# Strided values on shifted partitions, loaded in two pieces, and token rows stored tile by tile: a kernel of strided and local attention with a mixture of experts

## The chip, the cores and the metric

One core of a Trainium2 chip runs the whole program. The metric is the device time of one execution in microseconds. Of the kernel before, three runs gave 592.94, 595.64 and 595.68 us: the median is 595.64 us.

## The reference

Eight batches with eight heads of 576 tokens, 64 elements a head. The first four heads attend to the 32 latest tokens; the last four to earlier tokens of the same residue modulo 32 (18 of them). The 4608 token rows of 512 elements then go through a mixture of eight experts; each row goes to the one expert with the largest gate.

```python
scores = scale * np.matmul(q, k.transpose(0, 1, 3, 2))
rel = pos[:, None] - pos[None, :]
mask_local = (rel >= 0) & (rel < stride)
mask_strided = (rel >= 0) & (pos[None, :] % stride == pos[:, None] % stride)
...
attn = attn / (np.sum(attn, axis=-1, keepdims=True) + 1e-09)
return np.matmul(attn, v).astype(np.float32)
...
x = np.ascontiguousarray(attn_out.transpose(0, 2, 1, 3)).reshape(B * S, H * D)
logits = x @ w_gate + modality_bias[modality_id]
e_idx = np.argmax(logits, axis=1)
...
    h = np.maximum(x[mask] @ w1[e], 0.0)
    out[mask] = gate_w[mask, None] * (h @ w2[e])
```

## The kernel before

The work is cut into 32 units, eight for each of four pairs of batches, in turn a `Local` one (one local head of two batches) and a `Strided` one (two strided heads of one batch). A step n of the main loop (L1105) works on several units at once: the scores of unit n, the transposes (`turn`) of unit n - 2, the matmuls with the values (`values`) of unit n - 3, and in the middle of these the loads for later units. So each step has one unit of one kind in `scores`, and two steps make a pair with all loads of both kinds.

All loads of attention are issued by SP, in the order of the loop: for a local unit two pieces of `qk` (queries and keys) and two of `vv` (values), for a strided unit two pieces of `qks` and one load of `vs`. Each load of 128 partitions has 288 to 304 KB, and `vs` has 72 partitions with 4 KB each, 288 KB. `after_landing` (L777) makes a load wait until a matmul of the running step is done, so that not all loads are on their way at once: the second piece of `qk` or `qks` waits for the scores of the step, the first piece of the values for its transposes, the second piece for its value matmuls. `load_values(1)` of a strided unit loads nothing before the change.

In a strided unit a row of the values' matrix is a token of a residue: the matmul (L470) multiplies 72 rows, 18 tokens of each of four residues, of `vs` with `eb`. `eb` holds the transposed probabilities `en`, once for each residue and each time multiplied by a column of 0 and 1 from the constants `cf` (columns `C_T`), so that a residue meets its own 18 rows only (L453 to L460).

When the eight units of a pair are through, `finish_pair` (L480) transposes the results into token rows `xt` (nine tiles of 128 tokens), routes them, and stores them into `xd` in DRAM, from where the experts gather their tokens. For the first two pairs (`EARLY`) the stores go to the list `stores` and are issued by POOL (`store_rows`, L518), one per step of the main loop; for the other two pairs ACT issues them at once. `in_turn` (L780) keeps POOL's transfers in one order and makes each wait for a recent result of the units.

TensorE's order is written out by hand (`manual_schedule`, L1102); a scheduler orders the other engines by due times. The main loop ends near 165 us of the span. Behind it, and interleaved with the last units, the experts' feed-forward runs over slots of 384 tokens (`ffn`, L959), with split matmuls (`wh`, `wl`).

The loop's lines around the change are:

```python
        if 1 <= n <= nu:
            ins = units[n - 1].load_values(0)
            if n >= 2:
                after_landing(ins, units[n - 2].point)
...
        if n >= 3:
            units[n - 3].values()
        if 1 <= n <= nu:
            ins = units[n - 1].load_values(1)
            if ins and n >= 3:
                after_landing(ins, units[n - 3].valued)
```

Of the kernel before, what the change touches and what calls it, by code (L numbers as in the profile page):

```python
# [11 lines left out]
F32 = mybir.dt.float32  # L12
# [8 lines left out]
P = 128  # L21
# [24 lines left out]
TURNED = 4  # L46
EARLY, BEGIN = 2, 28
BIG = -float(2 ** 30)
SKIP = 2 ** 16
# [6 lines left out]
C_T = C_P + 1  # L56
C_F = C_T + 4
C_H = C_F + 4
# [26 lines left out]
def _constants():  # L85
# [6 lines left out]
    cf[:, C_F:C_F + 4] = P * np.arange(4)  # L92
    for t in range(4):
        cf[18 * t:18 * t + 18, C_T + t] = 1
    cb = np.zeros((P, M_N), np.float32)
# [88 lines left out]
def attention_moe(ctx: ExitStack, tc: tile.TileContext, a, out):  # L184
# [105 lines left out]
    for t in qzs:  # L290
        nc.gpsimd.memset(t[:], 0.0)


# [97 lines left out]
    class Strided:  # L391
# [11 lines left out]
        def load_values(self, part):  # L403
            if part == 0:
                self.vs = lp.tile([72, 8, 2, D], F32, tag="vs", name=f"vs{self.n}")
                return pin(nc.sync.dma_start(
                    self.vs.rearrange("p g h d -> p (g h d)"), a["vs"][self.b, self.pr]))

# [11 lines left out]
        def scores(self):  # L420
# [23 lines left out]
            nc.vector.reciprocal(sm[:], sm[:])  # L444
            self.en = lp.tile([P, 16, 18], F32, tag="ens", name=f"ens{n}")
            spots.append(nc.vector.tensor_tensor(self.en[:], ex[:], bc(sm), ALU.mult))

        def turn(self):
            n = self.n
            tp = pa(f"ts{n}").rearrange("p (g q) -> p g q", g=4)  # L450
            for g in range(4):
                self.point = turned_to(tp[0:72, g, :], self.en[:, 4 * g:4 * g + 4, :])
            self.eb = eb = lp.tile([72, 8, 4, 36], F32, tag="eb", name=f"eb{n}")  # L453
            src = tp[0:72].rearrange("p g (j x) -> p (g j) x", j=2)[:, :, 0:36]
            sh = [72, 8, 2, 36]
            nc.vector.tensor_tensor(
                eb[:, :, 0:2, :], src.unsqueeze(2).to_broadcast(sh),
                cf[0:72, C_T:C_T + 2].unsqueeze(1).unsqueeze(3).to_broadcast(sh), ALU.mult)
            for t in (2, 3):
                nc.scalar.activation(eb[:, :, t, :], src, AF.Copy, scale=cf[0:72, C_T + t:C_T + t + 1])  # L460

        def values(self):
            n, eb, vs, b = self.n, self.eb, self.vs, self.b
            for g2 in range(2):
                ot = pa(f"ot{n}{g2}")[:, :288]
                for g in (2 * g2, 2 * g2 + 1):
                    for j in range(2):
                        c = (g % 2) * 144 + 72 * j
                        for h in range(2):
                            self.valued = nc.tensor.matmul(  # L470
                                ot[64 * h:64 * h + 64, c:c + 72],
                                vs[:, 2 * g + j, h, :],
                                eb[:, 2 * g + j, :, 18 * h:18 * h + 18],
                                start=True, stop=True, skip_group_check=True,
                            )
                base = (b % 2) * S
                dst = self.xc[:, base:base + S].rearrange("p (q r) -> p r q", r=32)[:, 16 * g2:16 * g2 + 16, :]
                mark(nc.scalar.copy(dst, ot.rearrange("p (r q) -> p r q", r=16)))

    def finish_pair(bp, xt, xcs):  # L480
# [22 lines left out]
        for k0 in (0, 4, 8):  # L503
# [5 lines left out]
            if bp < EARLY:  # L509
                for k1 in range(k0, k0 + kn, 2):  # L510
                    stores.append(partial(store_rows, bp, xt, k1, min(2, 9 - k1)))
            else:
# [592 lines left out]
    for n in range(nu + 3):  # L1105
# [29 lines left out]
        pop(POPS)  # L1135
        if stores:
            stores.pop(0)()
        if n >= BEGIN:
# [75 lines left out]
```

## Time and profile before

| | |
|---|---|
| runs | 592.94, 595.64, 595.68 us |
| profiled execution | 598.07 us, span 596.3 us |
| TensorE busy | 570.7 us, 96% |
| VectorE (DVE), ScalarE (ACT), GpSimd (POOL) busy | 383.9, 328.8, 203.5 us |
| mean granted TensorE clock | 0.992 |
| moved by DMA | 103.50 MB, mean 174 GB/s |

Busy time counts neither the issue of DMAs nor waits. The time of the profiled execution includes 1.77 us around the span. In a timeline a row stands for several like instructions, and what is in brackets is the time in which the engine did nothing before the row, and what ended it. "issue" there means that the profile shows nothing for which the engine waited. SPq, ACTq and POOLq stand for instructions that issue DMAs.

### The profile page before, as it was taken

The numbers are of one execution on the slowest core, as the hardware profiler recorded it, in microseconds if no ns is written. First come the engines' busy times: TensorE is split into PE (matmuls) and PEld (weight loads), VectorE is DVE, ScalarE is ACT, GpSimd is POOL, SyncE is SP. The second block draws the span as 40 slices with busy tenths as digits, with TensorE's granted clock in tenths as the row PEclk, the third lists the DMA queues.
The fourth block names the chain that finished last, engine by engine and source line by source line (L and its number), as shares of the span: only waits on it lengthen the run. The fifth ranks groups of instructions, "written<-read, shape, count | busy, mean of one in ns | idle before, by whom it ended". The sixth has DMA issues, their size and how long they took to land.

```text
span 596.3 us, 13716 instructions
## 1 busy us (share of the span) xinstructions
PE 570.7 (96%) x5461; PEld 504.6 (85%) x5461; DVE 383.9 (64%) x925; ACT 328.8 (55%) x656; POOL 203.5 (34%) x194
## 2 busy tenths in 40 slices
PE   9889789889899999999999999999999999999995
PEld 5778777777789889899999898999989998998984
DVE  6885967966776795456476666657476666655432
ACT  5698878867574353445454454545454454545442
POOL 3010201102654326532264545544433444423121
PEclk9999999989899999999999999999999999999999
DMA  8997987968868515645555155432414256423421
GB/s 278 304 269 229 340 261 237 341 209 276 274 238 314 169 62 178 221 171 190 142 195 107 53 195 141 146 72 70 90 35 107 53 195 162 154 54 107 158 89 56
DMA packets 59547, 103.50 MB, mean 174 GB/s; under 512 B 33427, under 2 KB 33683, under 8 KB 55380
## 3 DMA queue, kind: packets, MB, share of 16 engines
q0 software_dynamic: 15904, 57.47, 28.2%
q1 hardware_dynamic: 40692, 39.85, 23.6%
q10 hardware_dynamic: 2880, 5.23, 2.5%
q8 instruction: 45, 0.74, 0.5%
q14 instruction: 26, 0.21, 0.1%
HBM read 98.28 MB, written 19.18 MB: 197 GB/s over the span
## 4 chain that ended last, share of the span: by engine, by line
PE 88%; issue 4%; DMA 4%; ACT 2%; POOL 1%; DVE 1%; POOLq 0%; ACTq 0%
PE h L968 34%; PE o L982 33%; DMA vs<-in_vs 3%; PE s L338 2%; PE ot L470 2%; PE ss L425 2%; PE o L373 2%; PE xs L217 2%; PE lg L532 1%; PE warm L204 1%; PE t L217 1%; PE xl L217 1%; PE xt L217 1%; DMA le<-ld,li 1%; PE ts L217 1%
## 5 line engine op out<-in xcount | busy, mean ns | idle before, releaser
L1004 DVE TENSOR_TENSOR wl<-raw,wh 128x512 fp32r<-128x512 f32 x192 | 126.3, 696 | 84.9 <-ACT wh L1003 78.1
L1003 ACT CAST wh<-raw 128x512 fp32r<-128x512 f32 x192 | 109.7, 622 | 115.2 <-PE o L982 101.2
L968 PE MATMUL h<-xh,wl 128*128 128x384 f32 x384 | 129.5, 337 | 0.0
L968 PE MATMUL h<-xl,wh 128*128 128x384 f32 x384 | 129.0, 336 | 0.0
L968 PE MATMUL h<-xh,wh 128*128 128x384 f32 x384 | 128.1, 337 | 0.3 <-ACT wh L1003 0.3
L982 PE MATMUL o<-wh,hl 128*128 128x512 f32 x288 | 113.7, 395 | 0.0
L982 PE MATMUL o<-wl,hh 128*128 128x512 f32 x288 | 113.5, 394 | 0.0
L982 PE MATMUL o<-wh,hh 128*128 128x512 f32 x288 | 112.8, 392 | 0.0
L971 ACT ACTIVATE hh<-h 128x384 fp32r<-128x384 f32 x96 | 47.2, 492 | 87.0 <-PE h L968 73.2
L973 DVE SCALAR_TENSOR_TENSOR hl<-h,hh 128x384 fp32r<-128x384 f32 x96 | 53.4, 556 | 57.5 <-ACT hh L971 57.1
L836 POOL DMA_INDIRECT raw<-in_w,wi x48 | 55.7, 1160 | 75.7 <-ACT hh L971 65.6
L968 PEld LDWEIGHTS h<-xh,wh 128*128 128x128 f32 x384 | 72.1, 188 | 4.4 <-ACT wh L1003 0.5
L968 PEld LDWEIGHTS h<-xl,wh 128*128 128x128 f32 x384 | 72.1, 188 | 3.7 <-issue 0.4
L804 POOL DMA_INDIRECT fx<-xd,le x36 | 44.3, 1231 | 82.0 <-DMA work<-work 21.4
L968 PEld LDWEIGHTS h<-xh,wl 128*128 128x128 f32 x384 | 72.0, 188 | 0.0
L982 PEld LDWEIGHTS o<-wh,hl 128*128 128x128 f32 x288 | 54.0, 188 | 11.5
L982 PEld LDWEIGHTS o<-wl,hh 128*128 128x128 f32 x288 | 54.1, 188 | 9.3
L982 PEld LDWEIGHTS o<-wh,hh 128*128 128x128 f32 x288 | 54.1, 188 | 8.9
L821 POOL DMA_INDIRECT le<-ld,li x36 | 39.0, 1082 | 58.1 <-DVE lo L565 26.0
L990 POOL DMA_INDIRECT out<-y,le x36 | 37.3, 1037 | 43.9 <-ACT y L989 37.6
L931 DVE COPY work<-fx 128x1536 uint16<-128x1536 uint16 x16 | 27.2, 1745 | 2.1 <-DMA fx<-xd,le 2.1
L524 POOL DMA_DIRECT2D xd<-xt x10 | 7.2, 725 | 62.1 <-ACT xt L487 39.9
(192 smaller groups left out, 771.2 us busy)
## 6 DMA issues: line engine op xcount, KB each, us to landing
vv<-in_vl SPq DMA_DIRECT2D x32, 292.5 KB
qks<-in_qks SPq DMA_DIRECT2D x32, 288.0 KB
qk<-in_qkl SPq DMA_DIRECT2D x16, 304.0 KB
qk<-in_qkl SPq DMA_DIRECT2D x16, 288.0 KB
vs<-in_vs SPq DMA_DIRECT2D x16, 288.0 KB
xd<-xt POOLq DMA_DIRECT2D x8, 512.0 KB
xd<-xt ACTq DMA_DIRECT2D x4, 1024.0 KB
raw<-in_w,wi POOLq DMA_INDIRECT x48
```

Of the source, the lines that this page charges most:

```text
L217: return nc.tensor.transpose(dst, src, ident)
L804: ins = in_turn(nc.gpsimd.indirect_dma_start(xt[:, h, :], None, xd[0:xrows, :], IOA(ap=le[:, h, 0:1], axis=0), **bounds))
L821: in_turn(nc.gpsimd.indirect_dma_start(le[:, h, :], None, ld[0:1 + last, :], IOA(ap=li[:, s, h:h + 1], axis=0)))
L836: ins = nc.gpsimd.indirect_dma_start(raws[j].rearrange("p f c -> p (f c)"), None, a["w"], IOA(ap=wi[:, s, j:j + 1], axis=0), bounds_check= ...
L931: pin(nc.vector.tensor_copy(rows[:, :, w, :], halves(xt)[:, :, :, w]))
L968: nc.tensor.matmul(hp, w[:, a1], x[:, c, :], start=(k == 0), stop=(k == 11))
L971: steps.append(nc.scalar.activation(hh[:], hp, AF.Relu))
L973: nc.vector.scalar_tensor_tensor(hl[:], hp, 0.0, hh.bitcast(F32), ALU.max, ALU.subtract)
L982: nc.tensor.matmul(os[h], hx[:, m], w[:, 512:1024], start=(f == 0 and i == 0), stop=(f == 7 and i == 2))
L990: outs.add(in_turn(nc.gpsimd.indirect_dma_start(out, IOA(ap=le[:, h, 0:1], axis=0), y[:], None, bounds_check=NT - 1, oob_is_err=False), True))
L1003: nc.scalar.copy(wh[:, c], raw[:, c])
L1004: nc.vector.tensor_tensor(wl[:, c], raw[:, c], wh[:, c].bitcast(F32), ALU.subtract)
```

## The change

Three things change. The values `vs` of a strided unit no longer lie on partitions 0 to 71 but on 32 to 103 in even strided units and on 24 to 95 in odd ones (`ROWS`), in two fixed buffers `vsp`. They are loaded by two DMAs: 64 rows on partitions 32 to 95, issued where the one load stood, and the other 8 rows on 96 to 103 or 24 to 31, issued behind the value matmuls of the step.

So that the probabilities lie on the same partitions, `en` is written into a buffer `enp` with 32 columns of zeros ahead of it, and the transpose takes 104 or 96 columns from there. `eb` and the matmul go over 104 or 96 partitions; the masks in `cf` are 0 in the rows ahead, and the buffers are set to zero by POOL at the start.

The token rows of the first two pairs are stored tile by tile, nine stores of 256 KB instead of four of 512 KB and one of 256 KB, one per step and two in each fourth step.

```diff
@@ -45,6 +45,7 @@
 WHEN = {1: 0, 3: 1, 5: 2, 7: 3}
 TURNED = 4
 EARLY, BEGIN = 2, 28
+ROWS = 32, 24
 BIG = -float(2 ** 30)
 SKIP = 2 ** 16
 
@@ -54,7 +55,7 @@
 C_SIO = C_RE8 + E
 C_P = C_SIO + NBP * LA
 C_T = C_P + 1
-C_F = C_T + 4
+C_F = C_T + 8
 C_H = C_F + 4
 C_N = C_H + TH
 
@@ -90,8 +91,9 @@
     cf[:, C_SIO:C_SIO + NBP * LA] = np.arange(NBP * LA)
     cf[:, C_P] = np.arange(P)
     cf[:, C_F:C_F + 4] = P * np.arange(4)
-    for t in range(4):
-        cf[18 * t:18 * t + 18, C_T + t] = 1
+    for i, r0 in enumerate(ROWS):
+        for t in range(4):
+            cf[r0 + 18 * t:r0 + 18 * t + 18, C_T + 4 * i + t] = 1
     cb = np.zeros((P, M_N), np.float32)
     cb[:, M_ID:M_ID + P] = np.eye(P)
     qi = np.arange(32)[:, None]
@@ -288,6 +290,10 @@
     for t in qds + ets:
         nc.vector.memset(t[:], 0.0)
     for t in qzs:
+        nc.gpsimd.memset(t[:], 0.0)
+    enp = zeros(2, [P, 32 + 288], "enp")
+    vsp = zeros(2, [104, 8, 2, D], "vsp")
+    for t in vsp + enp:
         nc.gpsimd.memset(t[:], 0.0)
 
 
@@ -401,10 +407,11 @@
             return pin(nc.sync.dma_start(self.qk[:, part, :], a["qks"][self.b, self.pr, :, S * part:S * part + S]))
 
         def load_values(self, part):
-            if part == 0:
-                self.vs = lp.tile([72, 8, 2, D], F32, tag="vs", name=f"vs{self.n}")
-                return pin(nc.sync.dma_start(
-                    self.vs.rearrange("p g h d -> p (g h d)"), a["vs"][self.b, self.pr]))
+            r0 = ROWS[self.n % 2]
+            r = (32, 96) if part == 0 else (96, 104) if r0 == 32 else (24, 32)
+            return pin(nc.sync.dma_start(
+                vsp[self.n % 2].rearrange("p g h d -> p (g h d)")[r[0]:r[1]],
+                a["vs"][self.b, self.pr, r[0] - r0:r[1] - r0]))
 
         def prep(self):
             self.qz = qz = qzs[self.n % 2]
@@ -442,25 +449,30 @@
             nc.vector.tensor_reduce(sm[:], ex[:], AX.X, ALU.add)
             nc.vector.tensor_scalar(sm[:], sm[:], 1e-9, None, ALU.add)
             nc.vector.reciprocal(sm[:], sm[:])
-            self.en = lp.tile([P, 16, 18], F32, tag="ens", name=f"ens{n}")
-            spots.append(nc.vector.tensor_tensor(self.en[:], ex[:], bc(sm), ALU.mult))
+            self.en = enp[n % 2]
+            spots.append(nc.vector.tensor_tensor(
+                self.en[:, 32:320].rearrange("p (i k) -> p i k", i=16), ex[:], bc(sm), ALU.mult))
 
         def turn(self):
-            n = self.n
+            n, r0 = self.n, ROWS[self.n % 2]
+            kn = r0 + 72
             tp = pa(f"ts{n}").rearrange("p (g q) -> p g q", g=4)
             for g in range(4):
-                self.point = turned_to(tp[0:72, g, :], self.en[:, 4 * g:4 * g + 4, :])
-            self.eb = eb = lp.tile([72, 8, 4, 36], F32, tag="eb", name=f"eb{n}")
-            src = tp[0:72].rearrange("p g (j x) -> p (g j) x", j=2)[:, :, 0:36]
-            sh = [72, 8, 2, 36]
+                c0 = 32 + 72 * g
+                self.point = turned_to(tp[0:kn, g, :], self.en[:, c0 - r0:c0 + 72])
+            self.eb = eb = lp.tile([104, 8, 4, 36], F32, tag="eb", name=f"eb{n}")
+            src = tp[0:kn].rearrange("p g (j x) -> p (g j) x", j=2)[:, :, 0:36]
+            sh = [kn, 8, 2, 36]
+            c0 = C_T + 4 * (n % 2)
             nc.vector.tensor_tensor(
-                eb[:, :, 0:2, :], src.unsqueeze(2).to_broadcast(sh),
-                cf[0:72, C_T:C_T + 2].unsqueeze(1).unsqueeze(3).to_broadcast(sh), ALU.mult)
+                eb[0:kn, :, 0:2, :], src.unsqueeze(2).to_broadcast(sh),
+                cf[0:kn, c0:c0 + 2].unsqueeze(1).unsqueeze(3).to_broadcast(sh), ALU.mult)
             for t in (2, 3):
-                nc.scalar.activation(eb[:, :, t, :], src, AF.Copy, scale=cf[0:72, C_T + t:C_T + t + 1])
+                nc.scalar.activation(eb[0:kn, :, t, :], src, AF.Copy, scale=cf[0:kn, c0 + t:c0 + t + 1])
 
         def values(self):
-            n, eb, vs, b = self.n, self.eb, self.vs, self.b
+            n, eb, vs, b = self.n, self.eb, vsp[self.n % 2], self.b
+            kn = ROWS[n % 2] + 72
             for g2 in range(2):
                 ot = pa(f"ot{n}{g2}")[:, :288]
                 for g in (2 * g2, 2 * g2 + 1):
@@ -469,8 +481,8 @@
                         for h in range(2):
                             self.valued = nc.tensor.matmul(
                                 ot[64 * h:64 * h + 64, c:c + 72],
-                                vs[:, 2 * g + j, h, :],
-                                eb[:, 2 * g + j, :, 18 * h:18 * h + 18],
+                                vs[0:kn, 2 * g + j, h, :],
+                                eb[0:kn, 2 * g + j, :, 18 * h:18 * h + 18],
                                 start=True, stop=True, skip_group_check=True,
                             )
                 base = (b % 2) * S
@@ -507,8 +519,8 @@
                 rows_of(c, k0)
             kn = min(4, 9 - k0)
             if bp < EARLY:
-                for k1 in range(k0, k0 + kn, 2):
-                    stores.append(partial(store_rows, bp, xt, k1, min(2, 9 - k1)))
+                for k1 in range(k0, k0 + kn):
+                    stores.append(partial(store_rows, bp, xt, k1, 1))
             else:
                 store_rows(bp, xt, k0, kn, nc.scalar)
         yield from routing
@@ -1133,8 +1145,9 @@
         if n + 2 < nu:
             units[n + 2].prep()
         pop(POPS)
-        if stores:
-            stores.pop(0)()
+        for _ in range(1 if n % 4 else 2):
+            if stores:
+                stores.pop(0)()
         if n >= BEGIN:
             issue(2)
         if n == nu + 1:
```

On SP, after the start-up the order of one pair of steps is this (`qk`, `vv`: the local unit's, `qks`, `vs`: the strided unit's; the DMAHW names are the eight counters of landed transfers, used in turn). Before:

```order
L406 DMA vs_765<-in_vs 72x1024 [waits DMAHW0_49,PE_49]
L305 DMA qk_791<-in_qkl 128x576 [waits DMAHW1_49,DVE_49,Activation_49]
L305 DMA qk_791<-in_qkl 128x608 [waits DMAHW2_49,PE_49]
L313 DMA vv_846<-in_vl 128x585 [waits DMAHW3_49,PE_49]
L313 DMA vv_846<-in_vl 128x585 [waits DMAHW4_49,PE_49]
L401 DMA qks_883<-in_qks 128x576 [waits DMAHW5_49,DVE_49,Activation_49]
L401 DMA qks_883<-in_qks 128x576 [waits DMAHW6_49,PE_49]
L406 DMA vs_924<-in_vs 72x1024 [waits DMAHW7_49,PE_49]
```

Now the same pair of steps reads:

```order
L412 DMA vsp_115<-in_vs 64x1024 [waits DMAHW3_49,PE_49]
L412 DMA vsp_115<-in_vs 8x1024 [waits DMAHW4_49,PE_49]
L311 DMA qk_795<-in_qkl 128x576 [waits DMAHW5_49,DVE_49,Activation_49]
L311 DMA qk_795<-in_qkl 128x608 [waits DMAHW6_49,PE_49]
L319 DMA vv_849<-in_vl 128x585 [waits DMAHW7_49,PE_49]
L319 DMA vv_849<-in_vl 128x585 [waits DMAHW0_49,PE_49]
L407 DMA qks_886<-in_qks 128x576 [waits DMAHW1_49,DVE_49,Activation_49]
L407 DMA qks_886<-in_qks 128x576 [waits DMAHW2_49,PE_49]
L412 DMA vsp_114<-in_vs 64x1024 [waits DMAHW3_49,PE_49]
L412 DMA vsp_114<-in_vs 8x1024 [waits DMAHW4_49,PE_49]
```

A pair has eight transfers where it had seven, the 8 rows stand between the 64 rows and the next `qk`, and every transfer now meets the counter of the same transfer of the pair before.

On POOL the stores of the first two pairs (`xd`) and the one product of the routing between them (`hv`) stand like this before:

```order
L524 DMA xd<-xt_116 128x2x512 x4
L624 TENSOR_TENSOR hv_1406<-hb_1404,val_1213 128x576
L576 COPY val_2005<-rt_sb 128x9
L524 DMA xd<-xt_116 128x512
L524 DMA xd<-xt_121 128x2x512 x4
L624 TENSOR_TENSOR hv_2198<-hb_2196,val_2005 128x576
```

and now:

```order
L536 DMA xd<-xt_124 128x512 x5
L636 TENSOR_TENSOR hv_1408<-hb_1406,val_1215 128x576
L588 COPY val_2007<-rt_sb 128x9
L536 DMA xd<-xt_124 128x512 x4
L536 DMA xd<-xt_129 128x512 x5
L636 TENSOR_TENSOR hv_2200<-hb_2198,val_2007 128x576
```

Ahead of the first `hv` stand five stores of one tile in place of four of two tiles, and four follow it in place of one. The orders of TensorE and VectorE are the same before and now.

## Rows read from the trace of the kernel before

**Rows 1.** The page: busy time of the engines, and one of the DMA queues.

```profile
PE 570.7 (96%) x5461; PEld 504.6 (85%) x5461; DVE 383.9 (64%) x925; ACT 328.8 (55%) x656; POOL 203.5 (34%) x194
...
q8 instruction: 45, 0.74, 0.5%
```

**Rows 2.** Busy time by stretch: length, engines, granted clock, DMA share, GB/s.

```profile
0.00:54.00 54.00, 48.27 (x1066) 37.72 (x1066) 40.27 (x115) 39.37 (x87) 7.77 (x14) 1.00 0.89 279
54.00:82.00 28.00, 22.60 (x605) 20.08 (x605) 20.34 (x79) 20.86 (x48) 5.13 (x7) 1.00 0.88 289
82.00:94.00 12.00, 11.79 (x224) 9.29 (x220) 8.35 (x25) 9.97 (x23) 0.00 (x0) 1.00 0.77 231
94.00:122.00 28.00, 23.76 (x613) 20.90 (x613) 23.48 (x98) 20.74 (x48) 4.80 (x7) 1.00 0.92 307
122.00:134.00 12.00, 12.00 (x211) 10.03 (x209) 8.16 (x47) 9.87 (x23) 0.00 (x0) 0.86 0.61 188
```

**Rows 3.** TensorE's timeline: start, us, line, tiles, count [idle before <- what ended it].

```profile
21.56 0.34 PE L470 MATMUL ot<-eb,vs 72*64 72x72 f32 x3 [0.85 <-issue]
...
27.39 0.80 PE L338 MATMUL s<-qk,qd 128*64 128x64 f32 x19 [1.86 <-issue]
...
43.67 1.22 PE L470 MATMUL ot<-eb,vs 72*64 72x72 f32 x32 [0.90 <-DMA vs<-in_vs]
...
73.08 1.43 PE L470 MATMUL ot<-eb,vs 72*64 72x72 f32 x31 [2.44 <-DMA vs<-in_vs]
...
80.14 0.46 PE L373 MATMUL o<-vv,et 128*64 128x65 f32 x9 [2.40 <-issue]
...
103.33 0.22 PE L338 MATMUL s<-qk,qd 128*64 128x64 f32 x1 [0.73 <-issue]
...
109.47 0.22 PE L373 MATMUL o<-vv,et 128*64 128x65 f32 x1 [1.15 <-issue]
...
121.17 0.34 PE L338 MATMUL s<-qk,qd 128*64 128x64 f32 x5 [2.16 <-issue]
```

**Rows 4.** DMA from 38 to 45 us in 40 slices: share in tenths, GB/s.

```profile
DMA  9687898999899999999999999999789999999999
GB/s 317 264 264 290 317 441 350 380 375 426 230 257 209 210 203 230 211 197 247 210 224 275 346 266 325 247 205 219 190 296 390 389 362 416 402 401 400 385 371 410
```

**Rows 5.** The chain that ended last, 30 to 80 us: start, us, what.

```profile
35.80 7.74 DMA vs<-in_vs
...
64.25 8.70 DMA vs<-in_vs
```

**Rows 6.** POOL: a row at the start; stores of all engines by group; POOL's fourth store.

```profile
0.73 2.06 POOL L291 MEMSET qz<- 128x1152 f32 x2 [0.29 <-POOLq L1206]
...
L524 POOL DMA_DIRECT2D xd<-xt x10: 596/722/974, 54.7 to 113.2; - x10
...
67.04 0.73 POOL L524 DMA_DIRECT2D xd<-xt  x1 [2.22 <-ACT xc L478]
```

**Rows 7.** SP: the vs loads by group (ns minimum/median/maximum, first and last start); two issues; a wait.

```profile
L406 SPq DMA_DIRECT2D vs<-in_vs x16: 325/326/1131, 13.1 to 151.1; - x16
...
64.25 0.37 SPq L406 DMA_DIRECT2D vs<-in_vs  x1
...
71.58 0.33 SPq L406 DMA_DIRECT2D vs<-in_vs  x1
...
SPq L305 <- DMA qk<-in_qkl: 3.3, 2, 2.2
```

**Rows 8.** Groups to 165 us by form: busy us, mean ns | idle before.

```profile
L217 PEld LDWEIGHTS t<-cf_sb,ex 128*128 128x128 f32 x80 | 8.4, 140 | 2.4 <-ACT exs L440 1.0 <-issue 0.5
L217 PEld LDWEIGHTS ts<-cf_sb,ens 128*72 128x72 f32 x64 | 6.1, 118 | 1.7 <-PE ss L425 1.3
L360 ACT COPY et<-t 64x512 f32<-64x512 f32 x32 | 18.5, 577 | 11.3 <-PE t L217 10.9
L487 ACT COPY xt<-xs 128x512 f32<-128x512 f32 x12 | 6.4, 592 | 0.3
```

## The prediction, made before the change was run

> **What bounds the kernel now.** I read the page first [rows 1]: TensorE is busy 570.7 of 596.3 us, so this order of work has 25.6 us in which TensorE does nothing, and no change of transfers can give more. Then the busy time by stretch [rows 2]: in the first four it lacks 5.7, 5.4, 0.2 and 4.2 us, in the fifth nothing. That is 15.5 of the 25.6 us; the other 10.1 lie in the 462 us behind 134 us, the end of attention and the experts, where there is next to no pause to win. The change touches attention alone, so it is judged by the pauses before 134 us.
>
> TensorE's timeline [rows 3] names them; the number in brackets is the idle time before the row. Eight pauses matter: 0.85, 1.86 and 0.90 us up to 44 us (3.61), 2.44 and 2.40 us between 70 and 81 us (4.84), 0.73, 1.15 and 2.16 us between 102 and 122 us (4.04). Together 12.49 us. Two of them end with a landing of `vs`. The chain of waits [rows 5] tells when those loads were issued: 35.80 and 64.25 us, 7.74 and 8.70 us before they ended the waits. The other six are marked "issue", nothing that the profile shows, but they are regular: from the row at 103.33 us to the last matmul before the row at 109.47 us the timeline counts 126 matmuls, each with its weight load, and from 21.56 us (its first row's start) to the pause before 27.39 us it counts 126 again. The page has a queue of kind "instruction" with 45 packets and 0.74 MB [rows 1], so 16 KB each. I read these pauses as TensorE waiting for its next block of program, which comes by the same DMA engines as the data.
>
> So attention is limited by how fast the DMA engines clear what is queued. Their share is 0.88 and 0.92 in the two stretches with token-row stores, and 0.77 and 0.61 in the stretches behind them [rows 2]: the load is uneven in time. It is also uneven in rate: between 39.75 and 43.1 us the engines are busy at 0.9 or more and move 237 GB/s in the mean of 19 slices; right after, from 43.25 us on, ten slices have 393 GB/s [rows 4]. The slow time ends as the `vs` issued at 35.80 us lands at 43.54 us [rows 5].
>
> **The change, part by part.**
>
> *Values over other partitions.* A load of 72 rows (295 KB) becomes 64 rows on partitions 32 to 95 and 8 rows beside them. No row shows such a load, so I bound it. At least nothing is saved, if the slow 3.3 us have another cause. If only the bytes of `vs` move at 237 instead of 393 GB/s, one load costs 1.24 instead of 0.75 us: 0.5 us saved. If all 3.3 us are its doing, the loss is 3.3 x (1 - 237/393) = 1.3 us. I take 0.5, since rows 4 do not say whose packets were moving. Four loads lie ahead of the pauses up to 44 us: 2 x 0.5 for the first two pauses, and 2 x 0.5 against a pause of 0.90, which caps it: 1.9 us. Three lie ahead of each of the other two groups: 1.5 us each.
>
> [...]
>
> *Token rows one tile at a time.* For each of the first two pairs, four stores of 512 KB and one of 256 KB become nine of 256 KB, one a step and two in each fourth step. Before, the ten stores are issued between 54.74 and 113.19 us, the fourth at 67.04 us [rows 6]. So at the pause at 70.6 us four are out, 2.10 MB; after, five tiles, 1.31 MB (the step with two has come). The 0.79 MB not yet there are 2.0 us of the engines' time at 393 GB/s [rows 4]. The later pause at 77.7 us is helped as well if its block of program was asked for while that queue stood: 2.0 us over the group. The same holds for the second pair. The delayed bytes move into 82 to 94 and 122 to 134 us, where the DMA share of 0.77 and 0.61 leaves 2.8 and 4.7 us free [rows 2]. Bounds: nothing (the pause moves along) and the whole 4.84 and 4.04 us.
>
> *What it adds.* Sixteen more issues on SP at 0.326 us [rows 7], 5.2 us on a queue that mostly waits for TensorE. The 8-row load waits until the matmuls of the strided unit before it are done, and the next `qk` load stands behind it. In the row at 43.67 us these matmuls follow the pause; without one they end about 1.2 us (their 32 at 1.22 us) after the point at which the 72-row load went. The piece that the next step but one needs is thus issued up to 1.2 us later. Where TensorE waited for `vs` (twice), this counts: between 0 and 2.4 us, I take 1.0.
>
> The four memsets on POOL: 2 x 1024 and 2 x 320 columns at the 2.06 us for 2 x 1152 [rows 6] are 2.4 us, so they end near 5.2 us (POOL starts them 0.73 + 2.06 us into the span), and behind them stand only two memsets of tiles for the experts' gathers; the first `vs` load is issued at 13.1 us [rows 7]. POOL's eight more stores cost 0.6 to 0.97 us each [rows 6], beside a POOL that does little else then. On TensorE the transposes take 104 or 96 columns instead of 72: weight loads of 128 columns take 140 ns, of 72 columns 118 [rows 8], so 64 times at most 22 ns, 1.4 us, in an engine part that overlaps the matmuls: nothing. `eb` is written on 104 or 96 partitions instead of 72 with as many columns: ACT copies of 512 columns take 577 ns on 64 partitions and 592 ns on 128 [rows 8], so 3% at most: nothing. The order of TensorE's and VectorE's instructions stays the same.
>
> *What is late next.* Between 94 and 122 us VectorE is busy 23.48 of 28 us [rows 2]. Taking 2.0 + 1.5 us out would ask it to be busy 96% of the stretch, with its waits for other engines still there. I count half: 1.8 us. Between 54 and 82 us VectorE and ACT stand at 20.3 and 20.9 of 28 us, so there I count all 3.5. Behind 134 us I count nothing; the look-ups and gathers there are paced by the steps, so they move forward with TensorE.
>
> *Sum.* 1.9 + 3.5 + 1.8 - 1.0 = 6.2 us. The profiled execution took 598.07 us (span 596.3), so it would be 591.9. It stood 2.43 us above the median of the runs shown (595.64); the same 6.2 us from the median give **589.4 us**.
>
> **The rivals.**
>
> *The pauses only move.* If the slow 3.3 us are not `vs`'s doing, or if the blocks of program come late whatever is queued, the first term goes and the stores give half: 2 x 1.0 in the first pair, 1.0 in the second after VectorE, less 1.0 for the later piece: 2.0 us, a median of 593.6. For it: six of eight pauses name no releaser, and the total bytes stay the same. Against it: the pauses gather where the DMA share is highest, and 82 to 94 us has next to none. Chance 0.24.
>
> *SP runs into its own landings.* In the order of SP's instructions each load waits for one of eight counters, so for the landing of the load eight places ahead. Before, seven loads make a pair of steps; after, eight, so each load waits for the same load of the pair before. Two successive `vs` issues stand 7.33 us apart [rows 7], and the landings took 7.74 and 8.70 us [rows 5]. SP, which now waits 3.3 us in two places for landed `qk` loads [rows 7], would be held 0.4 to 1.4 us on every pair of steps as long as a landing takes longer than a pair, and that is the point from which it decides. At 1.4 us on the eight pairs from 54 to 122 us this is 11.2 us, less the 6.2 gained: 5.0 us slower, 600.6. [...] Against it: smaller stores shorten the landings themselves, and a held SP has some 2 MB in flight, so the engines do not run dry. Chance 0.14.
>
> **How the numbers follow.** About 0.5%, 3 us, is what a measurement here tells from no change. The forecast holds for gains of 3 to 11 us and has 0.62: faster. Its own range is 584.5 to 592.6: at the fast end nearly all of the 12.49 us of pauses go. No change has 0.24 (the first rival), slower 0.14 (the second). To hold eight in ten, the range runs from 584.5 to 597.5: it takes in the first rival, and leaves out the greater part of the second and some 0.05 below.
>
> **What would show it.** In the profile after, the pauses at `ot` with a landing of `vs` are gone or under 0.5 us; the two groups of pauses in the store stretches shrink from 4.84 and 4.04 to about 1.3 and 2.2 us; the DMA share falls in the store stretches and rises behind them; the slow slices at full share before a `vs` lands disappear; TensorE's first `h` matmul comes 4 to 8 us earlier. It is wrong if the pauses keep their sum in other places, if SP's waits for landings grow past 10 us, or if the first `h` matmul comes earlier and the experts' part grows by as much.

## The result, and the profile after

The change took 589.88 us in the median of 20 runs (588.21 to 596.83), beside 595.70 us for the kernel before (20 runs). The ratio is 0.9903, 95% interval 0.9879 to 0.9928: 5.8 us less. Run once more, in another group, it had 0.9921 (0.9887 to 0.9955). The prediction said 589.4 us, 6.2 us less.

The profiled execution after took 588.97 us (span 587.0). The same stretches as in [rows 2], after (length, busy time of PE, PEld, DVE, ACT, POOL, granted clock, DMA share, GB/s):

```profile
0.00:54.00 54.00, 46.99 (x1064) 37.17 (x1065) 41.72 (x115) 39.12 (x86) 10.23 (x18) 1.00 0.85 279
54.00:82.00 28.00, 26.75 (x661) 23.54 (x658) 23.66 (x89) 23.67 (x56) 6.52 (x11) 1.00 0.90 313
82.00:94.00 12.00, 11.81 (x243) 9.38 (x242) 6.89 (x19) 10.01 (x24) 0.54 (x1) 1.00 0.69 224
94.00:122.00 28.00, 25.31 (x662) 22.19 (x662) 25.28 (x123) 24.09 (x56) 5.68 (x10) 1.00 0.92 323
122.00:134.00 12.00, 12.00 (x260) 9.96 (x258) 8.30 (x30) 9.72 (x23) 1.03 (x1) 1.00 0.74 240
```

TensorE now lacks 1.3 us instead of 5.4 in the second stretch and 2.7 instead of 4.2 in the fourth. The DMA share there is much the same (0.90 and 0.92, where it was 0.88 and 0.92), but the engines move more: 313 and 323 GB/s in place of 289 and 307. The last stretch had a granted clock of 0.86 before and has 1.00 now.

TensorE's timeline after, at the places that answer to [rows 3] (start, us, line, tiles, count, in brackets the idle time before the row and what ended it):

```profile
26.20 0.80 PE L344 MATMUL s<-qk,qd 128*64 128x64 f32 x20 [0.84 <-issue]
...
32.38 0.42 PE L333 MATMUL s<-cb_sb 128*128 128x256 bf16 x2 [1.73 <-issue]
...
76.42 0.57 PE L379 MATMUL o<-vv,et 128*64 128x65 f32 x12 [0.79 <-issue]
...
114.41 0.51 PE L344 MATMUL s<-qk,qd 128*64 128x64 f32 x10 [0.80 <-issue]
...
120.78 0.18 PE L432 MATMUL ss<-qks,qz 128*36 128x18 f32 x1 [1.10 <-issue]
```

No pause ends with a landing of the values any more, where there were 0.90 and 2.44 us. The pause of 2.40 us at the `o` matmuls is 0.79 us, the one of 2.16 us has gone down to 1.10. What is left above 0.6 us between 8 and 134 us are waits marked "issue" of at most 1.73 us. The longest of them is new: the pause of 1.86 us ahead of the row at 27.39 us before is 0.84 us now, but one of 1.73 us stands 126 matmuls behind it, where the kernel before had none.

The step from the pair of profiles to the result needs care. The first `h` matmul of the experts starts at 163.74 us before and at 153.82 us after, 9.9 us earlier, while the medians differ by 5.8. These two rows show the stretch up to it, of the kernel before,

```profile
0.00:163.74 163.74, 144.56 (x3229) 119.99 (x3229) 122.11 (x449) 120.59 (x274) 31.39 (x42) 0.98 0.85 274
```

and of the kernel after:

```profile
0.00:153.82 153.82, 139.05 (x3229) 116.41 (x3230) 122.81 (x450) 120.57 (x274) 36.19 (x54) 1.00 0.85 287
```

The same 3229 matmuls are busy for 144.56 us in one and 139.05 us in the other. Only 4.4 us of the 9.9 are idle time (19.18 and 14.77 us); the other 5.5 us are a shorter busy time, and the granted clock explains only a part of it. This execution of the kernel before had two drops of the clock that the execution after does not have: four microseconds from 122 us on with a mean of 0.62 (the rows are below) and four from 153 us on with 0.58. They cost some 1.6 us each, which is an estimate from these means. Another 1.2 us are the warm-up block at the start, first before and then after:

```profile
1.19 5.73 PE L204 MATMUL warm<-idle 128*128 128x512 bf16 x13 [1.19 <-DVE idle L197]
```

```profile
1.19 4.49 PE L206 MATMUL warm<-idle 128*128 128x512 bf16 x13 [1.19 <-DVE idle L199]
```

That gains nothing, since the kernel after then waits the longer for its first data: both start their 61st matmul at 8.7 us. For the last 1.1 us no row was found.

Cut at the start of the same matmuls (the 61st, the 1067th, the 2501st and the first `h`), the stretch shows where the gain lies. The kernel before:

```profile
8.72:54.12 45.40, 40.85 (x1014) 34.23 (x1011) 35.19 (x106) 36.66 (x83) 2.87 (x6) 1.00 0.91 280
54.12:122.37 68.25, 58.40 (x1436) 50.42 (x1436) 52.54 (x204) 51.63 (x119) 9.93 (x14) 1.00 0.88 286
122.37:163.74 41.37, 37.78 (x731) 31.85 (x731) 29.30 (x131) 29.48 (x70) 13.68 (x14) 0.92 0.77 248
```

The kernel after:

```profile
8.66:54.38 45.72, 41.00 (x1014) 34.25 (x1011) 35.51 (x107) 36.68 (x83) 2.64 (x6) 1.00 0.85 279
54.38:115.78 61.40, 58.38 (x1435) 50.47 (x1436) 51.31 (x200) 51.52 (x119) 12.74 (x22) 1.00 0.88 306
115.78:153.82 38.04, 33.31 (x731) 28.55 (x732) 29.78 (x136) 29.54 (x70) 13.22 (x14) 1.00 0.81 272
```

In the first part nothing is gained. In the middle part, with the store stretches, the same matmuls are busy for 58.4 us in both, and 6.8 us of idle time are gone. In the last part 3.3 us are gained although TensorE is idle for 1.1 us more: its busy time is 4.5 us shorter, and the two drops of the clock lie there.

### The profile page after: what moved, and what is told of

Read it like the earlier page. It is cut to its first block, busy times and chain, and to the rows that moved or that the text cites. A ratio compares the mean times of both kernels' runs of the same rounds, so it can differ in the third digit from the quotient of the medians.

```text
span 587.0 us, 13778 instructions
## 1 busy us (share of the span) xinstructions
PE 565.1 (96%) x5461; PEld 501.0 (85%) x5461; DVE 384.5 (66%) x925; ACT 328.7 (56%) x656; POOL 205.0 (35%) x206
## 3 DMA queue, kind: packets, MB, share of 16 engines
HBM read 98.29 MB, written 19.18 MB: 200 GB/s over the span
## 4 chain that ended last, share of the span: by engine, by line
PE 83%; DVE 7%; ACT 3%; issue 3%; DMA 2%; POOL 0%; ACTq 0%; SPq 0%; POOLq 0%; DVEq 0%
PE h L980 34%; PE o L994 34%; PE s L344 2%; PE o L379 2%; PE lg L544 1%; PE xs L219 1%; PE ot L482 1%; DMA fx<-xd,le 1%; PE ss L432 1%; PE xl L219 1%; DMA qks<-in_qks 1%; DVE mx L351 1%; DVE ex L352 1%; PE xt L219 1%; PE t L219 1%
## 5 line engine op out<-in xcount | busy, mean ns | idle before, releaser
L816 POOL DMA_INDIRECT fx<-xd,le x36 | 41.4, 1150 | 83.6 <-ACT wh L1015 35.4
L536 POOL DMA_DIRECT2D xd<-xt x18 | 10.0, 560 | 61.7 <-ACT xt L499 30.5
```

The source lines that it names most:

```text
L816: ins = in_turn(nc.gpsimd.indirect_dma_start(xt[:, h, :], None, xd[0:xrows, :], IOA(ap=le[:, h, 0:1], axis=0), **bounds))
```

## The experiments

Kernels sent together ran on one chip, and each ratio is against the kernel before on that chip. The groups below ran on four different chips, so between groups the ratios compare only roughly; the idle time of TensorE ahead of the first `h` matmul, from the profiles, is used beside them.

**The two parts alone.** First the values alone: the change with the old stores.

```diff
-                for k1 in range(k0, k0 + kn):
-                    stores.append(partial(store_rows, bp, xt, k1, 1))
+                for k1 in range(k0, k0 + kn, 2):
+                    stores.append(partial(store_rows, bp, xt, k1, min(2, 9 - k1)))
...
-        for _ in range(1 if n % 4 else 2):
-            if stores:
-                stores.pop(0)()
+        if stores:
+            stores.pop(0)()
```

> The values on shifted partitions in two loads, with the stores as before. Forecast of the prediction: its terms for the values alone, 1.9 + 1.5 + about 0.8 - 1.0 = 3.2 us of the whole gain, so about 592.5 us; the pauses of 0.85, 1.86 and 0.90 us up to 44 us shrink as in the full change, those from 70 to 122 us shrink by a third. Rival (the stores do it all): 595 us or more. Rival (the values do it all): 590 us.

Measured: 596.11 us, ratio 0.9954 (0.9922 to 0.9986), 2.8 us less. The pause at the `o` matmuls is still there, and one wait for the values, shorter than before:

```profile
70.57 1.22 PE L482 MATMUL ot<-eb,vsp 104*64 104x72 f32 x32 [0.79 <-DMA vsp<-in_vs]
77.20 0.57 PE L379 MATMUL o<-vv,et 128*64 128x65 f32 x12 [2.25 <-issue]
```

Then the stores alone, the opposite edit on the kernel before.

> The stores tile by tile, with the values on partitions 0 to 71 in one load. Forecast of the prediction: 2.0 us in the first pair and 1.0 in the second, so about 592.7 us; the pauses up to 44 us stay as before (3.6 us together), those of 2.44, 2.40 and 2.16 us shrink to under 1 us. Rival (the values do it all): 595 us or more.

Measured: 603.03 us, ratio 1.0040 (0.9998 to 1.0082). It is not faster. Its timeline shows that the pauses did not all shrink:

```profile
71.83 1.36 PE L470 MATMUL ot<-eb,vs 72*64 72x72 f32 x31 [1.15 <-ACT et L360]
...
79.37 0.51 PE L373 MATMUL o<-vv,et 128*64 128x65 f32 x9 [2.94 <-issue]
...
111.01 0.27 PE L373 MATMUL o<-vv,et 128*64 128x65 f32 x1 [2.31 <-issue]
```

The wait for `vs` near 70 us is gone, as forecast, though a pause of 1.15 us stays there. The pause behind it has grown from 2.40 to 2.94 us: thinner stores are later stores, and where it begins, at 76.4 us, eight tiles have been issued, while in the kernel before it was nine by 77.7 us. All the same, TensorE is idle for less time in the middle part, 7.8 instead of 9.9 us (table below). That the runs show no gain may be the clock's doing. Over the runs from which the ratio is taken the mean granted clock is 0.9847, and 0.9889 in the kernel before in this group; 0.42% is 2.5 us of some 599, about as much as the ratio lies above 1. That is an estimate and was not tried apart.

**Place or number of rows.** Two kernels undo one property of the values' loads each and keep the new stores. In the first the rows stay on partitions 0 to 71, still as 64 and 8.

```diff
-ROWS = 32, 24
+ROWS = 0, 0
...
-            r = (32, 96) if part == 0 else (96, 104) if r0 == 32 else (24, 32)
+            r = (0, 64) if part == 0 else (64, 72)
```

> The full change, but the values stay on partitions 0 to 71: 64 rows on 0 to 63 and 8 rows on 64 to 71, so sixteen DMA engines can share the 64 rows while half of the partitions take them. If the place of the rows is what counts, the slow slices at full share come back and the time lies 2 to 3 us above the full change, near 592.5 us. If the number of rows that sixteen divides is what counts, it equals the full change within 1 us.

Measured: 602.44 us, ratio 1.0057 (1.0025 to 1.0090). The second has the new place, with all 72 rows in one load.

```diff
-            r = (32, 96) if part == 0 else (96, 104) if r0 == 32 else (24, 32)
+            if part:
+                return None
+            r = (r0, r0 + 72)
```

> The full change, but all 72 rows of the shifted place come in one load where the 64 rows were issued. If the place of the rows is what counts, it equals the full change or is up to 1 us faster, since the late 8 rows fall away and SP has seven loads in a pair of steps again. If the division by sixteen is what counts, it lies 2 to 3 us above the full change.

Measured: 597.73 us, ratio 0.9998 (0.9959 to 1.0037). Neither half of the idea gives time without the other, and the first kernel is slower than the kernel before. The two expectations had been set against each other as if one had to be true, and both missed. Both kernels have the fixed buffers, the first has eight loads in a pair of steps, the second the wider transposes: none of these makes the gain.

**The loads by themselves.** So the disputed cost was measured alone: five groups of loads ahead of the kernel before, each behind the landing of the last.

```diff
+        for r0, rn, cols in ((0, 72, 1024), (32, 72, 1024), (0, 64, 1024), (32, 64, 1024), (0, P, 576)):
+            now = []
+            for i in range(12):
+                src = a["vs"][i // 2, i % 2, 0:rn] if rn < P else a["qks"][i // 2, i % 2, :, 0:576]
+                now.append(behind_groups(pin(nc.sync.dma_start(wide[r0:r0 + rn, i, 0:cols], src))))
+            group = now
```

> The kernel before, with five groups of twelve loads put ahead of everything, each group behind the landing of the one before and nothing beside them: 72 rows on partitions 0 to 71, 72 rows on 32 to 103, 64 rows on 0 to 63, 64 rows on 32 to 95, and 128 rows of 576 columns. It measures the rate of each shape alone. If the place decides: the first and third group move 220 to 240 GB/s (the slow slices' rate), the second 300 or more, the fourth near 390. If the division by sixteen decides: the first and second group are alike, about 300, and the third and fourth alike, near 390. The whole time grows by the groups, 50 to 70 us, and is of no interest.

Measured, one stretch from inside each group (the last two numbers are the DMA share and GB/s):

```profile
4.00:16.00 12.00, 1.54 (x7) 0.49 (x5) 0.78 (x2) 0.00 (x0) 1.43 (x2) 0.78 0.77 209
22.00:33.00 11.00, 0.00 (x0) 0.00 (x0) 0.00 (x0) 0.00 (x0) 0.00 (x0) 0.50 0.77 265
40.00:51.00 11.00, 0.00 (x0) 0.00 (x0) 0.00 (x0) 0.00 (x0) 0.00 (x0) 0.50 1.04 206
59.00:63.00 4.00, 0.00 (x0) 0.00 (x0) 0.00 (x0) 0.00 (x0) 0.00 (x0) 0.50 0.98 343
69.00:75.00 6.00, 0.00 (x0) 0.00 (x0) 0.00 (x0) 0.00 (x0) 0.00 (x0) 0.50 1.03 367
```

In order: 72 rows on 0 to 71, 209 GB/s; 72 rows on 32 to 103, 265; 64 rows on 0 to 63, 206; 64 rows on 32 to 95, 343; 128 rows, 367. Both properties limit. With 72 rows the share is 0.77 whatever the place, about twelve of sixteen engines. With 64 rows all engines are busy (shares of 1.04 and 0.98), but on partitions 0 to 63 they move 206 GB/s and on 32 to 95 they move 343: the place makes a factor of 1.67. Why the place matters was not shown.

**The one load with the old stores.** The shifted place in one load, without the new stores, on a third chip.

> The values alone, on the shifted place but in one load of 72 rows, with the stores as before. Beside the kernel with values alone in two loads (ratio 0.9954) it tells what the split is worth without the stores. If the place is what counts: 0.993 to 0.998. If the split over sixteen is needed: 0.999 or more.

Measured: 601.38 us, ratio 1.0025 (0.9992 to 1.0059). The split is needed here, too. The rates above do not explain all of it: by them one load of 72 rows takes 1.41 us on the old place and 1.11 us on the new one, 0.30 us less, and the two loads 0.55 us less. A part of the gain should have come, and none did; why is open.

**The late 8 rows, and the step of two stores.** In one group with the change itself:

> The change itself once more, beside the kernels of this group. If its gain is its own and not that of one chip or one moment, the ratio is again 0.988 to 0.993, with a mean granted clock above that of the kernel before. If the four kernels above came out worse only because of their chip, it falls back to 0.995 or more.

Measured: 594.51 us, ratio 0.9921 (0.9887 to 0.9955). Then the 8 rows right behind the 64:

```diff
+            if isinstance(units[n - 1], Strided):
+                units[n - 1].load_values(1)
         if n + 1 < nu:
             units[n + 1].masks()
...
-        if 1 <= n <= nu:
+        if 1 <= n <= nu and isinstance(units[n - 1], Local):
             ins = units[n - 1].load_values(1)
```

> The change with the 8 rows issued right behind the 64, without the wait for the step's value matmuls. The prediction charged 1.0 us (0 to 2.4) for the late piece: by it the time is 1 us below the change. If keeping transfers apart matters more than the late piece, it is equal or up to 2 us slower, with longer pauses for blocks of program.

Measured: 593.68 us, ratio 0.9893 (0.9842 to 0.9943). And the step with two stores moved:

```diff
-        for _ in range(1 if n % 4 else 2):
+        for _ in range(2 if n % 4 == 2 else 1):
```

> The change with the step of two stores moved by two (n % 4 == 2 in place of 0), so the nine stores of a pair come at other places of the same eight steps. If the gain comes from thinner stores and balanced values, it stays within 1.5 us of the change. If it comes from a lucky meeting of stores and blocks of program, it goes back to 0.995 or more of the kernel before.

Measured: 593.11 us, ratio 0.9898 (0.9859 to 0.9938). At this other place of the double step the gain stays. The late piece cannot be told from no cost: the intervals overlap. Both edits together, in the group on the third chip:

> The change with the 8 rows right behind the 64 and the double stores two steps later. If the two small gains seen (0.9893 and 0.9898 against 0.9903 and 0.9921 of the change) are real and add, 0.987 or less; if they are scatter, 0.989 to 0.993.

Measured: 596.50 us, ratio 0.9963 (0.9931 to 0.9995). Neither of the expected outcomes came: the ratio lies above both, and its interval lies above that of the change in the first group. In its profile the granted clock drops three times ahead of the first `h` (a mean of 0.96 over this stretch, 1.00 in the change). Whether the two edits together lose or that chip's executions had more drops is open; no kernel that clearly beats the change was found. The pause at the `o` matmuls, which the change itself has at 0.79 and 0.88 us, is longer in all three, in this order (8 rows at once, stores moved, both):

```profile
77.02 0.57 PE L379 MATMUL o<-vv,et 128*64 128x65 f32 x12 [1.86 <-issue]
```

```profile
77.38 0.57 PE L379 MATMUL o<-vv,et 128*64 128x65 f32 x12 [1.26 <-issue]
```

```profile
77.63 0.92 PE L379 MATMUL o<-vv,et 128*64 128x65 f32 x12 [2.10 <-issue]
```

**Without the loads of the values.** The values alone with the old stores, and of the values only the first two units' loads.

```diff
+            if self.n >= 2:
+                return None
             r0 = ROWS[self.n % 2]
```

> The stores as before, and of the strided values only those of the first two strided units are loaded: 14 of 16 loads, 4.1 MB, are left out, so the output is not the reference's. It bounds what any placing of these loads can give. By the prediction's upper price, 1.3 us a load for ten loads, at most the pauses they cause: 6 to 9 us below the kernel before. If the pauses come from the stores or the program blocks whatever the values do, under 3 us below.

Its whole time, 652.41 us (ratio 1.0899), says nothing here. Other values route the tokens in another way, and a further slot of experts, `c`, runs behind the fixed ones from 603 us on. The stretch up to the first `h` matmul can be read:

```profile
0.00:156.93 156.93, 142.40 (x3227) 118.83 (x3230) 122.71 (x450) 120.75 (x274) 33.50 (x46) 0.99 0.80 261
...
105.47 0.27 PE L379 MATMUL o<-vv,et 128*64 128x65 f32 x1 [2.02 <-issue]
```

Its idle time is 14.53 us. With nearly all values loads gone, a pause of 2.02 us stays in the second store stretch. By this one profile the place of these loads can give no more than 4.7 us of idle time, and between the 61st and the 1067th matmul no more than 1.2 us (3.3 us instead of 4.5). The change, with the thinner stores, has 14.77 us.

**The values alone once more**, on a fourth chip:

> The values alone once more (ratio 0.9954 on a chip on which the whole change was not run; the whole change had 0.9903 and 0.9921 on others). If the thinner stores add to the moved values, it is again 0.994 or more, with one pause of 2 us or more near 77 us. If the moved values do it all and the difference was the chip's, it is 0.992 or less.

Measured: 596.00 us, ratio 0.9947 (0.9907 to 0.9986), with a pause of 1.98 us at the `o` matmuls and one of 2.31 us at 32 us. So the values are worth about 0.5% alone, and the change 0.8 to 1.0%. The two never ran in one group, and the kernel with both edits, which has the thinner stores too, had 0.9963: that the thinner stores add time to the moved values is likely, but not shown.

**All profiles on one scale.** Up to the first `h` matmul, from the same view as the rows above, idle being the stretch less TensorE's busy time. The last three columns cut the idle time at the start of the 1067th and of the 2501st matmul, which the kernel before reaches at 54.12 and 122.37 us:

| kernel | first h, us | busy | idle | to the 1067th | middle | last |
|---|---|---|---|---|---|---|
| before | 163.74 | 144.56 | 19.18 | 5.7 | 9.9 | 3.6 |
| stores alone | 163.20 | 145.11 | 18.09 | 6.6 | 7.8 | 3.7 |
| 64 and 8 rows on 0 to 71, new stores | 161.84 | 143.08 | 18.76 | 7.5 | 6.5 | 4.8 |
| one load, new place, new stores | 167.26 | 148.13 | 19.13 | 6.8 | 7.7 | 4.6 |
| one load, new place, old stores | 163.64 | 143.16 | 20.48 | 7.5 | 9.1 | 4.0 |
| values alone, two profiles | 160.70, 160.03 | 144.80, 143.47 | 15.90, 16.56 | 5.5, 6.3 | 5.4, 5.4 | 5.1, 4.9 |
| change, two profiles | 153.82, 157.12 | 139.05, 142.23 | 14.77, 14.89 | 7.0, 5.4 | 3.0, 4.5 | 4.7, 5.0 |
| 8 rows at once | 157.16 | 141.07 | 16.09 | 6.8 | 4.7 | 4.6 |
| stores moved | 157.47 | 141.17 | 16.30 | 7.6 | 3.6 | 5.2 |
| both of these | 160.75 | 145.46 | 15.29 | 7.1 | 4.2 | 3.9 |

The idle column falls into two sets without overlap: 14.8 to 16.6 us with the values on the new place in two loads, 18.1 to 20.5 us without. The middle part makes this difference: 3.0 to 5.4 us in the one set and 6.5 to 9.9 us in the other, while the part up to the 1067th matmul shows none. Within each set the thinner stores go with less idle time in the middle part: 6.5 to 7.8 us against 9.1 and 9.9, and 3.0 to 4.7 us against 5.4. Each of these profiles is one execution.

## Why the prediction was right, point by point

*The bound.* It held that the pauses ahead of 134 us are what can be won, and that they are waits for what the DMA engines have queued. The pauses in the two store stretches shrank to 0.79 and 1.90 us (forecast 1.3 and 2.2). The waits for the values are gone, and the pause at the `o` matmuls is below 2.40 us in every kernel with the values on the new place in two loads, though with the values alone by little (2.25 and 1.98 us). That these pauses are waits for blocks of program was inferred from the count of matmuls; no run tried it apart. The profiles bear the regular places out. In the thirteen of the table above and of the kernel without the values' loads, 66 pauses above 0.5 us between the 61st and the 2700th matmul are marked "issue". Each of them lies at one of the places that are 126 matmuls apart, counted from the row at 21.56 us of [rows 3], or at most 11 matmuls ahead of it, whatever the kernel does beside.

*The values' term.* Alone the values gave 2.8 and 3.2 us (0.9954 and 0.9947 of about 599.5), and in idle time 2.6 to 3.3 us, where the prediction's terms make 3.2 us. But the gain did not come where the prediction put it, and that the sum came out is luck. The step that failed is "2 x 0.5 for the first two pauses, and 2 x 0.5 against a pause of 0.90, which caps it: 1.9 us". Between the 61st and the 1067th matmul, where these pauses lie, the change takes 45.72 us and the kernel before 45.40: nothing was gained. The pause moved on by one of the regular places, as the first rival said: 1.86 us became 0.84, and 1.73 us came 126 matmuls later. With nearly all of these loads left out, only 1.2 us of idle time go there, so by that profile 1.9 us were not to be had. In the middle part the values alone took away 4.5 us (9.9 to 5.4), about twice the 1.5 and about 0.8 us that the prediction gave them there.

The price of 0.5 us a load was near the measured rates: 295 KB at 209 GB/s is 1.41 us, and 262 KB at 343 with 33 KB at the same rate 0.86 us, 0.55 us less. But its reason was half of the truth. The prediction took it from the rate of the slow slices [rows 4] and put nothing down to the number of rows (of the nineteen slices that it read as 0.9 or more, the first has 0.8 and the last 0.7). Alone, the share of loads of 72 rows is 0.77; beside other loads and stores it is higher (0.88 and 0.92 in [rows 2]). Without the split nothing was gained, though the place was right.

*The stores' term.* This step failed in its size: "The 0.79 MB not yet there are 2.0 us of the engines' time", 2.0 us in the first pair and 1.0 us in the second, whether or not the values move. Alone the stores gave no time (1.0040); of idle time they took 1.1 us, 2.1 us in the middle part. The sum for the pause at 70.6 us held in the main: it is 1.15 us in the kernel with the stores alone, and no `vs` ends it. The words "is helped as well" for the pause at 77.7 us did not: it grew to 2.94 us. Nor did the delayed bytes move behind 82 us, but for one tile with the stores alone: eight of the nine tiles are issued by 76.4 us, and in the change the ninth at 79.3 us. With the values moved the pause at the `o` matmuls falls from 2.25 and 1.98 us to 0.79 and 0.88 us in the two profiles of the change, but it is 1.86, 1.26 and 2.10 us in the three kernels that differ from the change in one or two details. How much of it is the stores' doing is not settled. So the number 6.2 came out near 5.8 partly because terms that were too large stood in for others that were too small or missing.

*The missing term: the clock.* The prediction counted pauses at their length. A window of the kernel before, just behind its pause of 2.16 us (as above, the granted clock stands before the DMA share):

```profile
118.00:122.00 4.00, 1.84 (x45) 1.64 (x40) 3.36 (x17) 1.47 (x3) 0.00 (x0) 1.00 0.93 329
122.00:126.00 4.00, 4.00 (x46) 3.63 (x45) 3.28 (x29) 3.67 (x8) 0.00 (x0) 0.62 0.81 244
```

of the stores alone, around its pause of 2.31 us:

```profile
106.00:110.00 4.00, 2.16 (x63) 1.71 (x58) 3.43 (x19) 3.28 (x9) 0.54 (x1) 1.00 0.94 314
110.00:114.00 4.00, 2.99 (x57) 2.96 (x56) 2.33 (x10) 1.04 (x2) 0.88 (x1) 0.57 0.84 300
```

and of the values alone, behind its pause of 2.25 us:

```profile
74.00:78.00 4.00, 1.75 (x36) 1.36 (x36) 1.56 (x4) 2.14 (x5) 0.00 (x0) 1.00 0.96 359
78.00:82.00 4.00, 4.00 (x66) 3.45 (x62) 3.82 (x14) 0.60 (x2) 0.00 (x0) 0.57 0.58 173
```

Each time TensorE had been idle for more than 2 us, and then ran four microseconds with a mean granted clock near 0.6 (0.62, 0.57 and 0.57; from 123 to 126 us the kernel before had 0.50). It is no fixed rule: behind the pause of 2.40 us at 77.7 us the kernel before kept 1.00. In the thirteen profiles fourteen pauses above 2 us begin between 8 us and the first `h` matmul. Around the end of nine of them, within 2 us, such a drop begins, and five have none. Nine more drops stand elsewhere, one behind a pause of 1.98 us and eight between 141 and 159 us. The change, whose longest pauses are 1.73 and 1.80 us, has 1.00 throughout attention in both of its profiles. In the group on one chip its mean granted clock over all runs was 0.9936, that of the kernel before 0.9892; 0.44% of some 595 us is 2.6 us, of a gain of 4.7 us there (0.79% of 598.3). That is an estimate, since not all of the time scales with the clock.

*The costs.* The memsets took 2.5 us on POOL and end at 5.2 us, as said. The late 8 rows (1.0 us) were not to be seen, above. The transposes of 104 columns and the wider `eb` cost nothing that shows: VectorE is busy 122.81 instead of 122.11 us up to the first `h`, ScalarE 120.57 instead of 120.59.

*The rivals.* "The pauses only move" is true of the change up to 44 us and of one pause of the stores alone; in the middle part of the change they went. "SP runs into its own landings" did not happen. In SP's waits up to 165 us after, landings stand in only two rows:

```profile
SPq L407 <- DMA cb_sb<-in_cb: 1.3, 1, 1.3
...
SPq L311 <- DMA vv<-in_vl: 1.0, 2, 0.7
```

Before, SP waited 3.3 us for `qk` alone [rows 7]. That fits the argument against this rival, shorter landings; how long the landings took was not read. One load of 72 rows in place of the two, with seven transfers in a pair again, costs the whole gain: the kernels with it are at 0.9998 and 1.0025.

*The signs.* The waits for `vs`, the two groups of pauses and the earlier first `h` came as described (forecast 4 to 8 us; 9.9 in this pair of profiles, in which the clock helped, and 6.6 with the second profile of the change). The slow slices at full share are gone as well. From 38 to 45 us the kernel after has

```profile
DMA  9999898869797856967878898849999799998878
GB/s 418 350 299 331 328 398 313 265 247 323 300 306 162 258 232 275 332 249 275 286 298 336 322 376 256 202 188 309 362 360 372 305 343 330 303 304 238 251 290 316
```

and none of its forty slices has a share of 0.9 or more with at most 260 GB/s. In [rows 4] there are thirteen of them, and twelve with the values in two loads on partitions 0 to 71. The DMA share did not fall in the store stretches; the rate rose instead. Behind them the share went from 0.77 to 0.69 and from 0.61 to 0.74.

## What to carry to other kernels

A load that does not use all partitions should be looked at with two questions: how many of the sixteen DMA engines does its number of rows keep busy (a share of 0.77 with 72 rows here, of 1.04 and 0.98 with 64), and on which partitions do its rows lie? In the loads alone 64 rows on 32 to 95 moved 343 GB/s, 72 rows there 265, 64 rows on 0 to 63 only 206. In the whole kernel one of the two answers alone gave no time. And a term of a forecast should not be the sum of pauses in a stretch: a pause that is removed at one place can come back at the next (here 1.86 us became 0.84 and 1.73 us, and thinner stores made 2.94 of 2.40 us). The idle time between two matmuls that are the same in both kernels shows what is really gone.

## What had not been expected

Nine of fourteen pauses of TensorE above 2 us went with a drop of the granted clock (to a mean of 0.62, 0.57 and 0.57 over four microseconds in the three shown above), so such a pause can cost more than its length (an estimate: 1.6 us more behind one of 2.2 us). That the pause brings the drop was not tried apart. Up to the first `h` matmul the busy time of the same matmuls varied between 139.05 and 148.13 us over these profiles. And the same kernel before took 595.70, 598.33 and three times about 599.5 us in the medians of five groups, a spread of 3.9 us where the change gives 4.7 to 5.8.
